# Weight additions, splits and first transposes on TensorE, and one planned schedule with two buffer sets

## The chip, the cores and the metric

The kernel runs on one core of one Trainium2 chip. The metric is the device time of one execution in microseconds; lower is better. Before the change three timed runs gave 585.99, 586.38 and 587.47 us, median 586.38. The engines are named as in the profile: PE is TensorE, DVE VectorE, ACT ScalarE, POOL GpSimd, SP the engine that issues the DMAs. PE, DVE, ACT, POOL and SP each work through their own list in order.

## The reference, cut to what matters

```python
# attention: q, k, v of (8, 8, 576, 64), f32; 4 heads local, 4 strided
scores = (1.0 / np.sqrt(D)) * np.matmul(q, k.transpose(0, 1, 3, 2))
mask_local = (rel >= 0) & (rel < 32)
mask_strided = (rel >= 0) & (pos[None, :] % 32 == pos[:, None] % 32)
scores = np.where(masks, scores, -1e9)
attn = softmax(scores)
x = np.matmul(attn, v)                  # then heads side by side: (8, 576, 512)
# gated MLP: w_in (512, 1024), conv_w (3, 1024), w_out (1024, 512)
h = np.maximum(x @ w_in, 0.0)
conv_out = sum(conv_w[k] * shifted(h, k - 1) for k in range(3))
gate = 1.0 / (1.0 + np.exp(-conv_out))
out = (h * gate) @ w_out
```

`w_in`, `conv_w` and `w_out` come as float64 and reach the chip as pairs of 32-bit words; the kernel makes f32 of them itself.

## The kernel before

The batches are computed one after another. Each batch has four attention pairs (two heads each), then `mm1` (x times `w_in`, eight blocks f of 128 columns, two halves of 288 tokens), the gating of each f, and `mm2` (times `w_out`, four blocks m of 128 columns). All big products are done in three terms of a high and a low part (`xh`/`xl`, `wih`/`wil`, `gh`/`gl`, `woh`/`wol`): 192 products in `mm1` and 192 in `mm2` of a batch, each 128 x 128 by 288 columns (L387, L426).

An attention pair: scores on PE (L307), maximum and subtraction on DVE (L319, L320), exp on ACT (L322), sum and reciprocal on DVE (L323, L325), the normalisation `pn` on POOL (L326), a transpose of 32 x 32 blocks, either by DVE into `tt` with ACT copies from there (L329, L341) or by DVE directly (L344), the values on PE (L350), and the split of the result into `xh` (ACT, L364) and `xl` (DVE, L365).

Sixteen weight blocks (eight of `w_in`, eight of `w_out`, 512 KB each) are converted from float64 by `convert` and `from_f64`: one ACT pass (L245), five DVE passes (L246 to L254), an addition of head and tail on POOL (L256), the high part on ACT (L277) and the low part as a subtraction (L280) on POOL or DVE, which `SPLIT_W` chooses for each block. Two buffers each hold the words, `wa` and `wt`. `gl` of each f is the same helper `split` (L280); `SPLIT_G` puts six of eight on POOL.

A planner sets the order. Each operation has an engine, a duration, a due time and the operations it depends on; `order` walks through time and takes, on each engine, the ready operation that is due first. It is called twice: first the four attentions of batch 0 with four buffer sets and PSUM regions of their own, with four `w_in` blocks; then the rest, with two buffer sets. The due times are the tables at the top (`FIRST_AT`, `W_IN_AT` and so on). The planner knows no sharing between engines and gives a transfer a fixed duration.

Of the kernel before, what the change touches and what calls it, by code (L numbers as in the profile page):

```python
# [19 lines left out]
P = 128  # L20
W = 32
# [3 lines left out]
WAIT = 0.1  # L25
ACT_PENALTY = 0
PE_PENALTY = 1

FIRST = "q0 q1 w0 q3 v1 w1 w2 q2 w3 v2 v3 c0 v0"
SETUP = ['vav', 'v', 'ava', 'v']  # L30
WARM = 4
WARM_SCORES = [2, 4, 2, 4]
WARM_VALUES = [0, 5, 0, 9]
FIRST_AT = [19.3, 22.4, 23.0, 26.9]
SECOND_AT = [11.6, 24.2, 37.3, 76.0]
LATER_AT = [31.8, 33.4, 39.2, 37.7]
START = 28.0
PERIOD = 70.0
MM1_STEP = 3.5
MM2_AT = 39.3  # L40
MM2_STEP = 22.4
LOAD_Q = 82.1
LOAD_V = 20.4
W_IN_AT = [-37.0, 3.8, 71.4, 61.1, 22.5, 42.2, 40.1, 48.5]
W_OUT_AT = [1.2, -51.9, 2.7, -37.4, 27.2, 25.2, 41.3, 30.0]
SPLIT_W = "pppppppvppvppvpv"
SPLIT_G = "vppvpppp"
FIRST_SCALE = "aavaaaav"
FIRST_GATE = "vppppvpp"


class Plan:
# [6 lines left out]
    def op(self, engine, dur, at, fn, reads=(), writes=(), chain=(), table=None):  # L59
        i = len(self.ops)  # L60
        deps = set(chain)
        for key in reads:
            if key in self.last_write:
                deps.add(self.last_write[key])
        for key in writes:
            deps.update(self.readers.get(key, ()))
            if key in self.last_write:
                deps.add(self.last_write[key])
        for key in reads:
            self.readers.setdefault(key, set()).add(i)  # L70
        for key in writes:
            self.last_write[key] = i
            self.readers[key] = set()
        deps.discard(i)
        self.ops.append((engine, dur, at, fn, deps, table))
        return i

    def order(self, free, done):
        ops = self.ops
        n = len(ops)  # L80
        left = [0] * n
        users = [[] for _ in range(n)]
        ready = [0.0] * n
        end = {}
        lo = len(done)
        for i in range(lo, n):
            for d in ops[i][4]:
                if d < lo:
                    ready[i] = max(ready[i], self.after(done[d], d, i))
                else:  # L90
                    left[i] += 1
                    users[d].append(i)
        pool = {}
        for i in range(lo, n):
            if not left[i]:
                pool.setdefault(ops[i][0], []).append(i)
        out = []
        while True:
            best = None
            for e, c in pool.items():  # L100
                if not c:
                    continue
                t = max(free.get(e, 0.0), min(ready[i] for i in c))
                def key(i):
                    sw = e == "act" and ops[i][5] not in (None, self.table) or e == "pe" and ops[i][5] != self.kind
                    return (ops[i][2] + (ACT_PENALTY if e == "act" else PE_PENALTY) * sw, i)
                cand = min((i for i in c if ready[i] <= t), key=key)
                for i in c:
                    if ready[i] > t and key(i) < key(cand) and ready[i] < t + min(WAIT, 0.9 * ops[cand][1]):
                        cand = i  # L110
                        t = ready[i]
                        break
                if best is None or t < best[0]:
                    best = (t, e, cand)
# [4 lines left out]
            if e == "act" and ops[i][5] not in (None, self.table):  # L119
                self.table = ops[i][5]  # L120
                t += 1.29
            if e == "pe" and ops[i][5] != self.kind:
                self.kind = ops[i][5]
                t += 0.087
            end[i] = t + ops[i][1]
            free[e] = end[i]
            out.append((t, i))
            for u in users[i]:
                ready[u] = max(ready[u], self.after(end[i], i, u))
                left[u] -= 1  # L130
                if not left[u]:
                    pool.setdefault(ops[u][0], []).append(u)
        out.sort()
        return [i for _, i in out], end

    def after(self, t, d, i):
        a, b = self.ops[d][0], self.ops[i][0]
        if a == "dma":
            return t + 0.92
        if b == "dma":  # L140
            return t + 1.25
        if a == b:
            return t if a == "pe" else t + 0.13
        if b == "pe":
            return t + 0.15
        return t + (0.2 if a == "pe" else 0.15 if a == "act" else 0.08 if a == "pool" else 0.2 if b == "pool" else 0.13)

    def emit(self, free, done):
        order, end = self.order(free, done)
        for i in order:  # L150
            self.ops[i][3]()
        done.extend(end[i] for i in range(len(done), len(self.ops)))
# [3 lines left out]
def tile_banded_attention_gated_mlp(ctx, tc, qT, kT, vw, w_in, conv, w_out, mask, ident, out):  # L156
    nc = tc.nc
    B, NHP, D, _, S = qT.shape
    DM, FF = w_in.shape
# [3 lines left out]
    NF = FF // P  # L163
    NM = DM // P
# [8 lines left out]
    def attention_buffers(pool, i):  # L173
        return (pool.tile([P, 2, S], F32, name=f"q{i}"), pool.tile([P, 2, SP], F32, name=f"k{i}"),
                pool.tile([96, 2, NU, D], F32, name=f"v{i}"), pool.tile([96, 2, NU, 64], F32, name=f"pt{i}"),
                pool.tile([P, NU, 65], F32, name=f"t{i}"), pool.tile([P, NU, 64], F32, name=f"pn{i}"),
# [4 lines left out]
    tt = const.tile([P, NU, 64], F32, name="tt")  # L181
# [6 lines left out]
    NW = 2  # L188
    words = [const.tile([P, 4, P, 2], I32, name=f"ws{i}") for i in range(NW)]
    wa = [const.tile([P, 4 * P], I32, name=f"wa{i}") for i in range(NW)]  # L190
    wt = [const.tile([P, 4 * P], I32, name=f"wt{i}") for i in range(NW)]
# [4 lines left out]
    def slot(n):  # L196
        return n if n < NHP else n % NB

    def load_q(n, at):
        i, b, hp = slot(n), n // NHP, HPS[n % NHP]  # L200
        q, k = buffers[i][:2]
        op(Q, 0.82, at, lambda: nc.sync.dma_start(out=q[0:D], in_=qT[b, hp]), (), [("q", i)])
        op(Q, 0.82, at, lambda: nc.sync.dma_start(out=k[0:D, :, W:], in_=kT[b, hp]), (), [("k", i)])

    def load_v(n, at):
        i, b, hp = slot(n), n // NHP, HPS[n % NHP]
        v = buffers[i][2]
        op(Q, 1.23, at, lambda: nc.sync.dma_start(out=v, in_=vw[b, hp]), (), [("v", i)])

    def set_up(i, at):  # L210
        q, k, v, pt, t = buffers[i][:5]
        es = SETUP[i]

        def copy(e, dst, src, key, dv, da):
            if e == "a":
                op(A, da, at, lambda: nc.scalar.copy(dst, src), ["small"], [key])
            else:
                op(V, dv, at, lambda: nc.vector.tensor_copy(out=dst, in_=src), ["small"], [key])

        op(G, 0.09, -1, lambda: nc.gpsimd.memset(k[0:D, :, :W], 0.0), (), [("kpad", i)])  # L220
        copy(es[0], q[D:].rearrange("p h (u c) -> p (h u) c", c=64),
             small[D:, 0].unsqueeze(1).to_broadcast([64, 2 * NU, 64]), ("qid", i), 0.67, 1.05)
        if i == 1:
            op(Q, 0.87, at, lambda: nc.sync.dma_start(out=k[D:], in_=mask), (), [("kmask", i, h) for h in range(2)])
        elif i == 3:
            op(A, 1.1, at, lambda: nc.scalar.copy(k[D:], buffers[1][1][D:]), [("kmask", 1, 0)], [("kmask", i, h) for h in range(2)])
        else:
            op(G, 0.34, at - 0.5, lambda: nc.gpsimd.tensor_copy(out=k[D:, :, S:], in_=small[D:, 1, :W].unsqueeze(1).to_broadcast([64, 2, W])),
# [330 lines left out]
```

## Time and profile before

| what | value |
|---|---|
| median of the timed runs | 586.38 us |
| profiled execution | 583.28 us, its span 581.5 us |
| PE busy | 523.2 us (90%) |
| DVE busy | 416.1 us (72%) |
| ACT busy | 348.6 us (60%) |
| POOL busy | 169.2 us (29%) |
| mean granted TensorE clock | 0.944 |
| moved by DMA | 52.19 MB, mean 90 GB/s |

The span runs from the first to the last instruction; some 1.8 us of the execution lie around it. A share over the span mixes stages: the slices of the page show a start of some 140 us with a TensorE clock of 0.5 to 0.9 in places, then a long stretch at full clock. A row of a group reads: line, engine, operation, out<-in, shape, count, busy us, mean ns, idle time before it and who ended that. A row of the waits reads: who waited, for whom, us in total, times, longest.

### The profile page before, as it was taken

How to read it: one execution, taken by the hardware profiler on the slowest of the kernel's cores; microseconds unless marked ns; L12 is line 12 of the kernel's file. 1: busy time of each engine (PE TensorE's matmuls, PEld its weight loads, DVE VectorE, ACT ScalarE, POOL GpSimd, SP SyncE). 2: the span in 40 equal slices, each digit the busy share in tenths (PEclk: the TensorE clock that was granted, in tenths of full speed). 3: DMA queues.
4: the chain of work that ended last, by engine and by line, in shares of the span. 5: the costliest groups of instructions: out<-in, count | busy, mean ns of one | idle time of the engine just before them, and what ended most of it. 6: DMA issues, size and time to landing. Idle time of an engine off the chain costs nothing.

```text
span 581.5 us, 15083 instructions
## 1 busy us (share of the span) xinstructions
PE 523.2 (90%) x6558; PEld 498.2 (86%) x6558; DVE 416.1 (72%) x587; ACT 348.6 (60%) x661; POOL 169.2 (29%) x148
## 2 busy tenths in 40 slices
PE   5468855798998999999999999999999999899997
PEld 2348854697997999999998999899999999799997
DVE  5596999998697666875787678767777668733830
ACT  4395685566676448663874477545765386535731
POOL 5434676674023111321033012311232103300220
PEclk9566967889999999999999999999999999999999
DMA  8994213445202460066006530355015600210001
GB/s 194 228 214 108 66 56 110 141 145 163 68 1 81 130 160 1 4 182 163 24 1 143 151 77 2 85 152 134 1 32 155 165 22 1 83 42 22 1 35 47
DMA packets 24178, 52.19 MB, mean 90 GB/s; under 512 B 2480, under 2 KB 10736, under 8 KB 24112
## 3 DMA queue, kind: packets, MB, share of 16 engines
q1 hardware_dynamic: 24112, 51.23, 33.0%
q8 instruction: 51, 0.84, 0.6%
q14 instruction: 15, 0.12, 0.1%
HBM read 41.79 MB, written 9.44 MB: 88 GB/s over the span
## 4 chain that ended last, share of the span: by engine, by line
PE 44%; DVE 22%; ACT 11%; issue 4%; POOL 0%; POOLq 0%; DVEq 0%; ACTq 0%
PE m L426 24%; PE m L387 13%; DVE c L404 8%; DVE c L409 6%; PE s L307 4%; ACT c L398 4%; ACT gh L277 2%; PE s L350 2%; ACT c L407 2%; DVE gl L280 1%; DVE wt L250 1%; DVE xl L365 1%; ACT pt L341 1%; ACT h L393 1%; ACT xh L364 1%
## 5 line engine op out<-in xcount | busy, mean ns | idle before, releaser
L387 PE MATMUL m<-xh,wil 128*128 128x288 f32 x512 | 153.1, 299 | 5.7 <-DVE wil L280 3.8
L426 PE MATMUL m<-gl,woh 128*128 128x288 f32 x512 | 153.7, 300 | 3.7 <-POOL gl L280 3.3
L426 PE MATMUL m<-gh,wol 128*128 128x288 f32 x512 | 152.6, 298 | 4.9 <-DVE wol L280 2.9
L426 PE MATMUL m<-gh,woh 128*128 128x288 f32 x512 | 155.5, 304 | 1.3 <-issue 1.3
L387 PE MATMUL m<-xh,wih 128*128 128x288 f32 x512 | 153.4, 300 | 2.0 <-DVE xl L365 1.5
L404 DVE SCALAR_TENSOR_TENSOR c<-h,cw,c 128x576 f32<-128x576 f32 x128 | 121.1, 952 | 44.7 <-ACT c L398 44.4
L387 PE MATMUL m<-xl,wih 128*128 128x288 f32 x512 | 153.1, 299 | 0.0
L280 POOL TENSOR_TENSOR gl<-c,gh 128x576 fp32r<-128x576 f32 x48 | 71.5, 1490 | 202.0 <-ACT gh L277 192.1
L426 PEld LDWEIGHTS m<-gl,woh 128*128 128x128 f32 x512 | 97.4, 190 | 9.1 <-POOL gl L280 7.5
L387 PEld LDWEIGHTS m<-xh,wil 128*128 128x128 f32 x512 | 98.2, 192 | 6.1 <-DVE wil L280 4.0
L426 PEld LDWEIGHTS m<-gh,wol 128*128 128x128 f32 x512 | 97.5, 190 | 4.0 <-DVE wol L280 3.4
L426 PEld LDWEIGHTS m<-gh,woh 128*128 128x128 f32 x512 | 97.3, 190 | 4.2 <-issue 1.5
L387 PEld LDWEIGHTS m<-xh,wih 128*128 128x128 f32 x512 | 98.2, 192 | 2.8 <-DVE xl L365 1.7
L387 PEld LDWEIGHTS m<-xl,wih 128*128 128x128 f32 x512 | 98.1, 192 | 0.0
L341 ACT COPY pt<-tt 32x288 f32<-32x288 f32 x160 | 68.8, 430 | 24.8 <-DVE tt L329 16.1
L326 POOL TENSOR_TENSOR pn<-t,sm 128x576 f32<-128x576 f32 x32 | 38.2, 1203 | 145.7 <-DVE sm L325 141.6
L277 ACT CAST gh<-c 128x576 fp32r<-128x576 f32 x64 | 43.0, 671 | 41.0 <-DVE c L409 39.3
L409 DVE TENSOR_TENSOR c<-h,c 128x576 f32<-128x576 f32 x58 | 54.7, 944 | 15.0 <-ACT c L407 14.1
L393 ACT ACTIVATE h<-m 128x288 f32<-128x288 f32 x128 | 50.5, 405 | 22.6 <-PE m L387 21.3
L432 ACT COPY o<-m 128x288 f32<-128x288 f32 x64 | 24.8, 398 | 58.5 <-PE m L426 54.2
L407 ACT ACTIVATE c<-c 128x576 f32<-128x576 f32 x64 | 43.4, 678 | 11.7 <-DVE c L404 11.0
L398 ACT ACTIVATE c<-h,cw 128x576 f32<-128x576 f32 x62 | 48.1, 775 | 1.5
(71 smaller groups left out, 590.2 us busy)
## 6 DMA issues: line engine op xcount, KB each, us to landing
v<-in_dram SPq DMA_DIRECT2D x32, 432.0 KB, 4.0
q<-in_dram SPq DMA_DIRECT2D x32, 288.0 KB, 5.0
k<-in_dram SPq DMA_DIRECT2D x32, 288.0 KB, 5.7
out_dram<-o SPq DMA_DIRECT2D x32, 288.0 KB, 2.2
ws<-in_dram SPq DMA_DIRECT2D x16, 512.0 KB, 3.7
k<-in_dram SPq DMA_DIRECT2D x1, 304.0 KB, 6.7
small<-in_dram SPq DMA_DIRECT2D x1, 32.0 KB, 2.1
cwords<-in_dram SPq DMA_DIRECT2D x1, 24.0 KB, 10.6
```

Source lines behind the costliest of these rows:

```text
L277: op(A, ta, at, lambda: nc.scalar.copy(hi(), src), [skey], [(key, "h")])
L280: lambda: eng.tensor_tensor(out=lo(), in0=src, in1=hi().bitcast(F32), op=ALU.subtract),
L326: op(G, 1.11, at + 5.5, lambda: nc.gpsimd.tensor_tensor(out=pn, in0=t, in1=sm.unsqueeze(2).to_broadcast([P, NU, 64]), op=ALU.mult), [("t", ...
L341: op(A, 0.333, at + 7.5, lambda dst=dst, j=j, p=p: nc.scalar.copy(dst, tt[j:j + 32, :, 32 * p:32 * p + 32]), ["tt"], [key])
L387: nc.tensor.matmul(ps, a[:, c, fs], x[:, c, tok], start=(n == 0 and m == 0), stop=(n == NC - 1 and m == 2))
L393: op(A, 0.291, at + 1.5 * t + 1.7, lambda ps=ps, t=t: nc.scalar.activation(out=h[:, 1 + t * H2:1 + t * H2 + H2], in_=ps, func=AF.Relu), [( ...
L398: op(A, 0.67, at + 3.6, lambda: nc.scalar.activation(out=c_, in_=h[:, 0:S], func=AF.Copy, scale=cw[:, f:f + 1]), kh + ["cw"], [kc])
L404: op(V, 0.73, at + 3.6 + 0.8 * kk, lambda kk=kk: nc.vector.scalar_tensor_tensor(out=c_, in0=h[:, kk:kk + S], scalar=cw[:, kk * NF + f:kk * ...
L407: op(A, 0.57, at + 6, lambda: nc.scalar.activation(out=c_, in_=c_, func=AF.Sigmoid), [kc], [kc], table=1)
L409: op(ge, 0.67 if ge == V else 1.36, at + 6.7, lambda: (nc.vector if ge == V else nc.gpsimd).tensor_tensor(out=c_, in0=h[:, 1:S + 1], in1=c ...
L426: nc.tensor.matmul(ps, a[:, f, ms], g[:, f, tok], start=(f == 0 and n == 0), stop=(f == NF - 1 and n == 2))
L432: op(A, 0.291, at + 3 * t + 3, lambda ps=ps, tok=tok: nc.scalar.copy(o[:, tok], ps), [("M", mi)], [("o", oi, t)])
```

## The change

Four things change together.

1. **Weights.** `_words` lays each weight block out in order, so that a row of a partition is 4 KB in one piece. There are three word buffers, two of `wa` and `wt`, one of the tail `wl`, and the first three `w_in` blocks land in `misc`, which later holds `h`, `c` and `o`. Head and tail are added by PE in PSUM: a product of the head with a unit matrix (f32), then one of the tail (f32r). For blocks marked "a" in `SPLIT_W` (10 of 16) PE also subtracts the high part, by four products with a negative unit matrix, and ACT copies the low part out; for the others DVE subtracts.
2. **First transposes.** For the four pairs of batch 0 and the first two of batch 1 the normalised probabilities go into `pad`, 18 products with a unit matrix transpose them into PSUM (`turn`), and three ACT copies bring them to `pt`, zeros with them.
3. **GpSimd** keeps the normalisation, in place, and `gl` of two in eight f (one in batch 0).
4. **One plan.** Everything is planned at once, with two buffer sets throughout, PSUM regions `psR` for attention and `mm`, a lock between DVE and POOL, a TensorE that is slow after a pause, transfers by their bytes, new durations and new due times.

```diff
+PASSES = 0
+AHEAD = 4.0
+RATE = 205.0
-SPLIT_W = "pppppppvppvppvpv"
-SPLIT_G = "vppvpppp"
+SPLIT_W = "aavvvaaaaaaaavvv"
+SPLIT_G = "vvvpvpvv"
+FIRST_SPLIT_G = "vvvvvpvv"
+TURNED = 2
+FIRST_GATE = "vvvvvvvv"
...
+                if ops[i][6]:
+                    lock["dve"] = end[i] + 0.03
+                    lock["pool"] = end[i]
...
+    NWS, NWA, NWT, NWL = 3, 2, 2, 1
...
     def slot(n):
-        return n if n < NHP else n % NB
+        return n % NB
...
-        op(G, 0.2 if short else 1.23, at, lambda: nc.gpsimd.tensor_tensor(out=w, in0=w, in1=af, op=ALU.add), [ka], [kt])
...
+        def whole():
+            nc.tensor.matmul(ps, eye, t, start=True, stop=False)
+            nc.tensor.matmul(ps, eyer, tail, start=False, stop=not last)
+        op(A, 0.615, at, lambda: nc.scalar.copy(hi(), parts(t)), [kt], [(key, "h")])
+        op(T, 1.1, at, whole, [kt, kl, "unit", "eyer"], [("M", mi)], table=4)
+        if last:
+            def rest():
+                for x in range(4):
+                    nc.tensor.matmul(ps[:, P * x:P * x + P], negr, hi()[:, x, :], start=False, stop=x == 3)
+            op(T, 0.3, at, rest, [(key, "h"), "negr"], [("M", mi)])
+            op(A, 0.59, at, lambda: nc.scalar.copy(lo(), parts(ps)), [("M", mi)], [(key, "l")])
+        else:
+            op(V, 0.69, at, lambda: nc.vector.tensor_tensor(out=lo(), in0=parts(ps), in1=hi().bitcast(F32), op=ALU.subtract),
+               [("M", mi), (key, "h")], [(key, "l")])
...
+        def turns():
+            for u in range(n_u):
+                for e in range(2):
+                    o = ps[0:96, 128 * u:128 * u + 128].rearrange("p (h x) -> p h x", h=2)[:, :, 32 * e:32 * e + 32]
+                    nc.tensor.matmul(o, pad[:, u0 + u, 32 - 32 * e:128 - 32 * e], unit[:, e, :], start=True, stop=True)
...
+        turned = spread is None
+        pn = pad[:, :, 32:96] if turned else t
...
+def _words(w, n):
+    y = np.ascontiguousarray(w).view(np.int64).reshape(n, 4, P, -1, P)
+    return np.ascontiguousarray(y.transpose(3, 0, 2, 1, 4).reshape(-1, P, 4 * P))
```

**SP, the loads of batch 0 from the third pair on.** Before, every pair has its own set (58, 66, 98 and 106 are q of the four sets):

```order
L202 DMA q_98<-in_dram 64x1152
L203 DMA k_99<-in_dram 64x2x576
L208 DMA v_100<-in_dram 96x1152
L272 DMA ws_81<-in_dram 128x4x256
L208 DMA v_108<-in_dram 96x1152
L260 DMA cwords<-in_dram 128x48
L208 DMA v_60<-in_dram 96x1152
```

After it the same queue, from the load of `q` of pair 3 into set 1 (65 to 67) to the last `v` of batch 0:

```order
L312 DMA q_65<-in_dram 64x1152
L317 DMA k_66<-in_dram 64x2x576
L312 DMA q_58<-in_dram 64x1152
L317 DMA k_59<-in_dram 64x2x576
L322 DMA v_60<-in_dram 96x1152
L377 DMA ws_98<-in_dram 128x1024
L377 DMA ws_99<-in_dram 128x1024
L312 DMA q_65<-in_dram 64x1152
L322 DMA v_67<-in_dram 96x1152
```

The last `v` of batch 0 now stands behind q and k of batch 1's first pair, the next weight blocks and q of its second pair; 24 other loads (8024 KB) are ahead of it.

**PE, around the first product of `mm1`.** Before, the values of the last two pairs, then `mm1` (m_550 is its first PSUM buffer):

```order
L350 MATMUL sF_116<-pt_101,v_100 64x64 x18
L350 MATMUL sF_117<-pt_109,v_108 64x64 x18
L387 MATMUL m_550<-xh,wih 128x288
L387 MATMUL m_550<-xh,wil 128x288
L387 MATMUL m_550<-xl,wih 128x288
```

After the change the same place, with additions (L393, L394; r_95 and r_96 hold the buffers of `mm`), transposes (L439) and values (L508) between:

```order
L393 MATMUL r_96<-wt_103,eyes 128x512
L394 MATMUL r_96<-wl_104,eyer 128x512
L508 MATMUL r_95<-pt_61,v_60 64x64 x18
L439 MATMUL r_93<-eyes,pad 96x2x32 x16
L545 MATMUL r_95<-xh,wih 128x288
L545 MATMUL r_95<-xh,wil 128x288
L545 MATMUL r_95<-xl,wih 128x288
L439 MATMUL r_93<-eyes,pad 96x2x32 x2
L393 MATMUL r_96<-wt_102,eyes 128x512
L394 MATMUL r_96<-wl_104,eyer 128x512
L508 MATMUL r_93<-pt_68,v_67 64x64 x18
```

The first products of `mm1` moved ahead of the last pair's values, and each weight block puts two products into PE's list, each of which waits for a DVE result; all blocks use the one tail buffer wl_104.

**POOL, from the gating of batch 0 on.** Before (49 onwards of its list; wt are the converted words, wil and wol low parts):

```order
L409 TENSOR_TENSOR c_541<-h_538,c_541 128x576
L326 TENSOR_TENSOR pn_63<-t_62,sm_65 128x576
L280 TENSOR_TENSOR gl<-c_541,gh 128x576
L280 TENSOR_TENSOR wil<-wt_86,wih 128x4x128
L409 TENSOR_TENSOR c_542<-h_539,c_542 128x576
L256 TENSOR_TENSOR wt_85<-wt_85,wa_83 128x512
L280 TENSOR_TENSOR gl<-c_542,gh 128x576
L280 TENSOR_TENSOR wil<-wt_85,wih 128x4x128
```

After the change POOL's list for the whole of that stage (the fifth and sixth pairs into `pad`, one `gl`, the last two pairs in place; the last row's second is the first pair of batch 2):

```order
L479 TENSOR_TENSOR pad<-t_62,sm_64 128x9x64
L479 TENSOR_TENSOR pad<-t_69,sm_71 128x9x64
L417 TENSOR_TENSOR gl<-misc,gh 128x576
L479 TENSOR_TENSOR t_69<-t_69,sm_71 128x9x64
L479 TENSOR_TENSOR t_62<-t_62,sm_64 128x9x64 x2
```

Additions, low parts and gates left POOL's list; the additions went to PE, the gates and most `gl` to DVE.

More of the change, by code (lines that the diff above doesn't have):

```diff
@@ new lines, in attention @@
+        if not turned and sum(spread):
+            op(V, 0.777, at + 6.8, lambda: nc.vector.transpose(out=tt, in_=pn), [("t", i)], ["tt"])
+        keys = []
+        if turned:
+            keys = [("pt", i, 0, 0, 0), ("pt", i, 0, 0, 1), ("pt", i, 0, 1, 0)]
+            turn(n, full, ks[0], 0, 4, keys[0], at + 7)
+            turn(n, full[:, 512:], ks[1], 4, 4, keys[1], at + 7.6)
+            turn(n, full, ks[0], 8, 1, keys[2], at + 8.2)
+            keys += [("pt", i, h, e, p) for h in range(2) for e in range(2) for p in range(2) if ("pt", i, h, e, p) not in keys]
@@ L333, in attention @@
+        for h in range(0 if turned else 2):
             for e in range(2):
@@ L377, in mm1 @@
         h, c_ = hs[hi], cs[hi]
+        sg = FIRST_SPLIT_G[f] if early else SPLIT_G[f]
         for t in range(2):
```

559 lines of the change are left out of this document (326 added, 233 removed).

## The prediction, as put on record before the run

> **What bounds the kernel now.** I read the windows first, cut at the first `mm1` product (48.04 us) and at the first `mm1` product of batch 1 (149.11 us). Columns: busy time of each engine with its instructions, granted clock, DMA share, GB/s.
>
> ```profile
> core 0: us, PE busy (x) PEld busy (x) DVE busy (x) ACT busy (x) POOL busy (x), PEclk, DMA share, GB/s
> 0.00:48.04 48.04, 26.28 (x462) 17.72 (x463) 31.13 (x55) 28.54 (x55) 22.72 (x40) 0.66 0.86 203
> 48.04:149.12 101.08, 78.80 (x961) 73.60 (x962) 95.11 (x120) 62.40 (x118) 59.42 (x44) 0.84 0.38 111
> 149.12:581.50 432.38, 418.11 (x5138) 406.92 (x5136) 289.84 (x413) 257.67 (x489) 87.03 (x65) 1.00 0.27 72
> 10.00:40.00 30.00, 16.21 (x312) 11.51 (x314) 20.72 (x39) 18.05 (x37) 11.81 (x11) 0.54 0.99 230
> ```
>
> There are three stages with three limits. From 10 to 40 us the DMA engines are full (share 0.99, 230 GB/s). From 48 to 149 VectorE is busy 95.1 of 101.1 us. After 149 TensorE is busy 418 of 432 us. The waits of TensorE say what is left there, in the third stage and then in the second:
>
> ```profile
> PE s L307 <- DVE xl L365: 3.9, 6, 0.7
> PE m L426 <- issue: 2.8, 2, 1.5
> PE m L426 <- POOL gl L280: 2.8, 9, 1.0
> ...
> PE s L350 <- ACT pt L341: 8.8, 4, 5.0
> PE m L387 <- DVE wil L280: 3.8, 1, 3.8
> PE s L307 <- DVE xl L365: 3.3, 2, 2.4
> PE m L426 <- DVE wol L280: 2.9, 2, 2.6
> PE m L387 <- POOL wil L280: 1.8, 1, 1.8
> ```
>
> The third stage has some 10 us of waits in 432. The second has 23.6 (the rows shown and four small ones), and more is lost to half clock and to a VectorE that GpSimd holds up. The timeline shows the holding:
>
> ```profile
> 67.67 1.92 POOL L280 TENSOR_TENSOR gl<-c,gh 128x576 fp32r<-128x576 f32 x1
> ...
> 68.25 1.63 DVE L246 TENSOR_SCALAR wa<-wa 128x512 f32<-128x512 f32 x1
> ...
> L246 DVE TENSOR_SCALAR wa<-wa x16: 407/424/1630, 13.0 to 133.9; 128x512 f32<-128x512 f32 x16
> L248 DVE TENSOR_SCALAR wa<-wa x16: 385/427/1628, 14.0 to 134.8; 128x512 int32<-128x512 int32 x16
> L250 DVE SCALAR_TENSOR_TENSOR wt<-ws,wa x16: 677/834/1901, 14.5 to 136.7; 128x512 int32<-128x512 int32 x16
> L252 DVE TENSOR_SCALAR wa<-wt x16: 368/416/1530, 15.8 to 138.4; 128x512 int32<-128x512 int32 x16
> L254 DVE SCALAR_TENSOR_TENSOR wa<-ws,wa x16: 675/683/1755, 16.2 to 138.8; 128x512 f32<-128x512 uint32 x16
> L404 DVE SCALAR_TENSOR_TENSOR c<-h,cw,c x16: 800/806/1856, 56.4 to 113.5; 128x576 f32<-128x576 f32 x16
> L409 DVE TENSOR_TENSOR c<-h,c x2: 742/1223/1704, 62.6 to 96.7; 128x576 f32<-128x576 f32 x2
> ```
>
> A clamp that takes 407 ns alone took 1630 ns when it began during a GpSimd pass; the last rows give shortest/median/longest in ns. GpSimd is busy 59 us of that stage.
>
> **Part 1, the first 48 us.** The loads are the limit. Counted from SP's order, the last `v` of batch 0 stands behind 8456 KB (8.66 MB) in the new kernel: the same q, k and v, six weight blocks, and q and k of batch 1's first pairs. The stream reaches that amount when 10 to 40 us have gone by at 230 GB/s and the first 10 us at the row below:
>
> ```profile
> 0.00:10.00 10.00, 6.59 (x88) 3.19 (x88) 5.31 (x8) 3.58 (x4) 7.57 (x26) 1.00 0.75 166
> ...
> L341 ACT COPY pt<-tt 32x288 f32<-32x288 f32 x68 | 29.2, 429 | 7.6 <-DVE tt L329 6.7
> ...
> 48.04 0.61 PE L387 MATMUL m<-xh,wih 128*128 128x288 f32 x1 [1.52 <-DVE xl L365]
> ```
>
> 1.66 + 6.9 = 8.56 MB by 40 us, so 8.66 MB at about 40.4. Behind it come the values (1.1 to 2.2 us), the xh copy and the xl subtraction: full `mm1` from about **44** instead of 48.04. The weights now come in rows of 4 KB, which no row prices; between no gain and the same bytes 20% faster lie 0 to 3 us, and I take none. The two buffer sets instead of four make q, k and v wait for earlier pairs; the tightest is `v` of pair 3, which SP issues after the values of pair 1; by the chain of that pair (q and k landed, softmax, transposes: about 32 us) 1.5 MB of earlier issues, some 7 us, are then still under way, so these waits are hidden under the transfers. Without that cover each would cost its own length. Eight ScalarE copies of 0.43 us a pair become three from PSUM, which no row shows; priced between none and the eight they replace they save at most 3.4 us a pair, hidden under the same loads.
>
> **Part 2, from 44 us to `mm1` of batch 1.** With the additions and splits on TensorE, GpSimd keeps in this stage only four normalisations and one `gl`. VectorE's list there (102 rows) at the shortest durations above: ten conversions of 0.407 + 0.385 + 0.677 + 0.368 + 0.675 = 2.51 us are 25.1; 16 convolution passes of 0.80 are 12.8; 36 other full passes (gates, `gl`, `lo`, softmax, xl, transposes) at 0.742 are 26.7; small ones 1.2; together 66 us, plus about 7 us held by the five GpSimd passes (1.2 to 1.9 each): 73 us, where 95 were. So VectorE stops being the bound, and TensorE becomes it. Its list goes by these rows (chain and timeline):
>
> ```profile
> 525.59 12.74 PE m L387 x96
> 499.31 2.22 PE s L307 x144
> 513.60 2.25 PE s L350 x72
> ...
> 146.62 0.40 PE L426 MATMUL m<-gh,woh 128*128 128x288 f32 x1
> 146.85 0.30 PE L426 MATMUL m<-gh,wol 128*128 128x288 f32 x1
> 146.99 0.29 PE L426 MATMUL m<-gl,woh 128*128 128x288 f32 x1
> ```
>
> A product is 12.74/96 = 0.1327 us; two scores take 2.22, two values 2.25; a change of type costs about 0.1 (0.23 to the next start instead of 0.13). No row shows the new matmuls. Values write 64 partitions and cost 2.25/36 = 0.0625 us for 64 f32 columns, scores write 32 and cost half of it, so I take a full-width one at 0.125 per 64 columns; below stands 0.0625. The addition is then 8 x 0.125 + 512/288 x 0.1327 = 1.24 us (low end 0.74), a split 0.24, a transpose 0.125. From 44 us: 375 products 49.8, six scores 6.7, four values 4.5, 36 transposes 4.5, 11 additions 13.6, eight splits 1.9, some 50 changes of type 5.0: **86 us** (78 at the low end). Three us of waits, the choice between none and the 23.6 of before, nearer to none because the conversions run well ahead, give 44 + 86 + 3 = **133** in place of 149.1: 16 us gained. What hides the new 25 us on TensorE is that it stood still or at half clock for them; without that cover they would be paid in full.
>
> The Trainium skill ("FP8 and Floating Point Precision", TensorE Precision Notes) says that true FP32 takes four passes through the array; four times 0.236 us would make an addition's f32 half an estimated 0.94 us, which speaks for the upper end and would take 0.7 us off the sum; no run shows it yet.
>
> **Part 3, the other seven batches.** The products are the same, and scores now stand further behind the values whose xl they wait for, and six of eight `gl` are on VectorE. Of 3.9 + 2.8 of such waits I take 4 us; the bounds are 0 and 8.
>
> **Sum.** 583.3 (the profiled execution: 581.5 and 1.8 around it) - 16 - 4 = 563.3. The three timed runs have their median 3.1 above the profiled one, so the forecast is **566**.
>
> **Rivals.** *VectorE stays the bound.* If its list is stretched as before (L404 took 1126 ns on average there, 1.4 times the shortest), 66 becomes 92 us; then 44 + 92 and some 6 us for the last values and products give 142, and 583.3 - 7 - 4 + 3 = 575. For it: GpSimd still has work; against: 5 passes instead of 44 instructions.
>
> ```profile
> L404 DVE SCALAR_TENSOR_TENSOR c<-h,cw,c 128x576 f32<-128x576 f32 x16 | 17.9, 1126 | 0.7 <-ACT c L398 0.7
> ```
>
> *Half clock stays.* After waits TensorE ran at half clock:
>
> ```profile
> 115.54 0.61 PE L426 MATMUL m<-gh,wol 128*128 128x288 f32 x1 [2.63 <-DVE wol L280]
> 115.95 0.44 PE L426 MATMUL m<-gl,woh 128*128 128x288 f32 x1
> 116.19 0.44 PE L426 MATMUL m<-gh,woh 128*128 128x288 f32 x1
> ...
> 117.00:121.00 4.00, 4.00 (x19) 4.00 (x18) 3.96 (x5) 3.02 (x5) 4.00 (x3) 0.50 0.18 63
> ```
>
> Products 0.24 apart until 121 us: a wait of 2.6 us cost some 2.7 more. At the old mean clock of 0.84, 86 us become 102, the end 149, and the time 582. Against: the conversions fill TensorE's pauses. The Trainium skill ("TensorE: Matmul & The Clock Gate", What's actually happening) lets the clock fall only after an idle window of about 3.4 us; by it this wait would have been free, but the trace shows that it was not, and the trace decides.
>
> *More than forecast.* Transposes and additions at the low end (-8), loads 3 us sooner, no waits (-3), 8 us later on: 583.3 - 30 - 8 + 3 = 548. For it: all engines have room once GpSimd is out of the way.
>
> *Slower.* TensorE works in order, and there is one buffer `wl` for the tail of a weight block: an addition that waits for VectorE holds every product behind it, and VectorE's next tail waits for that addition. At 2.9 us (the wait on `wol` above) for each of 11 conversions it would be 32 us, and 598; it decides from (20 + 0.3% of 586)/11 = 2.0 us each. Against: before, TensorE's waits on weights shown above are four, in 16 conversions.
>
> **How the numbers follow.** Forecast 0.56 (558 to 573), VectorE 0.13 and half clock 0.09 (573 to 583), more 0.15, slower 0.05, nothing 0.02. The range 552 to 580 leaves out half of "more", the slower end and a little of the second. A measurement of this kernel tells about 0.3% from no change; faster 0.92, same 0.03 (the last and a sliver of the half-clock case), slower 0.05.
>
> **What would show it.** Part 1: the first full `mm1` at 41 to 46 us with the loads at 0.9 and more before it. Part 2: VectorE below 85% and TensorE above 90% busy from there to `mm1` of batch 1, which begins between 128 and 138; L351 (L250 before) with its median near 0.69 us instead of 0.83; additions of 0.7 to 1.3 us. Part 3: 424 to 432 us from there to the end. Wrong would be: loads that stand still in the first 40 us, long waits of TensorE for `wl`, or a clock below 0.9 in the second stage.

## The result, and the profile after

| | before | changed |
|---|---|---|
| time, median | 586.18 us (584.05 to 587.47, 4 runs) | 623.15 us (620.79 to 624.90, 4 runs) |
| ratio to before | | 1.063 (95%: 1.058 to 1.068) |
| profiled execution, its span | 583.28, 581.5 us | 622.13, 620.2 us |
| first full `mm1` | 48.04 | 54.35 |
| from there to `mm1` of batch 1 | 101.1 | 95.1 |
| from there to the end | 432.4 | 470.8 |

The forecast was 566 us; the kernel became 6.3% slower. The windows of the changed kernel, cut at the same places (the first `mm1` product after the last values of batch 0, and the first of batch 1), and two cuts in the start; columns as before:

```profile
0.00:54.35 54.35, 37.62 (x616) 29.86 (x616) 31.03 (x63) 20.63 (x37) 7.61 (x23) 0.94 0.78 194
54.35:149.44 95.09, 88.37 (x1098) 78.02 (x1095) 69.42 (x116) 59.85 (x110) 6.33 (x6) 1.00 0.41 110
149.44:620.20 470.76, 432.31 (x5138) 408.82 (x5136) 291.22 (x444) 261.80 (x493) 45.05 (x38) 1.00 0.25 67
10.00:40.00 30.00, 23.69 (x433) 18.56 (x430) 16.38 (x37) 9.74 (x19) 3.87 (x9) 0.89 0.86 212
25.00:30.00 5.00, 3.75 (x48) 2.46 (x49) 2.78 (x9) 0.88 (x2) 1.15 (x1) 0.50 0.68 142
```

The second stage is as forecast in kind: VectorE 69.4 of 95.1 us, TensorE 88.4. The loss is in the third, where TensorE has the same 5138 instructions and 38 us more. Its waits there, in the changed kernel:

```profile
PE r L545 <- ACT misc L551: 25.6, 51, 0.5
PE r L585 <- ACT misc L591: 7.7, 15, 0.5
PE r L459 <- issue: 1.2, 1, 1.2
```

66 waits of 0.5 us for ScalarE's copy out of PSUM, of a kind that the waits of before do not have. One of them in the timeline (start, duration, engine, line; in brackets the idle time and what ended it):

```profile
218.43 0.30 PE L545 MATMUL r<-xl,wih 128*128 128x288 f32 x1
218.56 0.29 PE L545 MATMUL r<-xh,wih 128*128 128x288 f32 x1
218.69 0.29 PE L545 MATMUL r<-xh,wil 128*128 128x288 f32 x1
218.82 0.29 PE L545 MATMUL r<-xl,wih 128*128 128x288 f32 x1
219.15 0.41 ACT L551 ACTIVATE misc<-r 128x288 f32<-128x288 f32 x1 [0.73 <-PE r L545]
219.62 0.40 PE L545 MATMUL r<-xh,wih 128*128 128x288 f32 x1 [0.50 <-ACT misc L551]
219.85 0.29 PE L545 MATMUL r<-xh,wil 128*128 128x288 f32 x1
```

The group for t = 0 ends with the product at 218.43. ScalarE's ReLU of that group could start at about 218.75, but starts at 219.15, right after the third product of the *next* group (218.82 + 0.29); and the fourth product of that group waits until the ReLU has ended. Two groups that share no element of PSUM wait for each other, both ways. From 218.82 to 219.85 pass 1.03 us for two steps that otherwise take 0.13 each: 0.77 us lost.

What the two groups share is a tile. The kernel before had four `mm` buffers that were PSUM tiles of their own; in the changed one they are halves of two tiles of 1024 columns (`psM` from `psR[2]` and `psR[3]`). The waits written into the program show the same. In the pair of groups below, which fills the two halves of `r_96`, the wait for ScalarE (Activation_49) stands at the fourth product of the second group:

```
962 L545 MATMUL r_96<-xh,wih 128x288
963 L545 MATMUL r_96<-xh,wil 128x288
964 L545 MATMUL r_96<-xl,wih 128x288
965 L545 MATMUL r_96<-xh,wih 128x288 [waits Activation_49]
```

The other direction stands there too. TensorE counts up a semaphore (a counter on which other engines wait), and in this pair it does so only at the third product of the second group, by 15: for the twelve products of the first group and these three. The ReLU of the first group waits for that count, so it cannot start when its own group ends. In the program with tiles of their own (below) `mm1` counts up at the twelfth product of a group.

### The profile page after: what moved, and what is told of

It reads as the page before. It is cut to its first block, busy times and chain, and to the rows that moved or that the text cites. A ratio compares the mean times of both kernels' runs of the same rounds, so it can differ in the third digit from the quotient of the medians.

```text
span 620.2 us, 15601 instructions
## 1 busy us (share of the span) xinstructions
PE 558.3 (90%) x6846; PEld 516.7 (83%) x6846; DVE 391.7 (63%) x622; ACT 342.3 (55%) x639; POOL 59.0 (10%) x66
## 4 chain that ended last, share of the span: by engine, by line
PE 86%; ACT 8%; DMA 3%; issue 2%; DVE 0%; POOL 0%; SPq 0%; ACTq 0%; POOLq 0%
PE r L545 34%; PE r L585 33%; PE r L508 6%; PE r L459 5%; ACT misc L551 4%; PE r L439 3%; PE r L393 2%; DMA q<-in_dram 2%; ACT misc L591 1%; DMA misc<-in_dram 1%; PE r L400 1%; PE r L394 1%; ACT t L473 1%; ACT pt L441 0%; ACT misc L557 0%
## 5 line engine op out<-in xcount | busy, mean ns | idle before, releaser
L545 PE MATMUL r<-xh,wih 128*128 128x288 f32 x512 | 157.2, 307 | 28.9 <-ACT misc L551 27.6
L585 PE MATMUL r<-gh,woh 128*128 128x288 f32 x512 | 156.3, 305 | 9.1 <-ACT misc L591 8.2
L585 PE MATMUL r<-gh,wol 128*128 128x288 f32 x512 | 150.9, 295 | 0.2 <-issue 0.2
L545 PE MATMUL r<-xl,wih 128*128 128x288 f32 x512 | 150.8, 294 | 0.0
L545 PE MATMUL r<-xh,wil 128*128 128x288 f32 x512 | 150.7, 294 | 0.0
L585 PE MATMUL r<-gl,woh 128*128 128x288 f32 x512 | 150.7, 294 | 0.0
L563 DVE SCALAR_TENSOR_TENSOR misc<-misc,cw 128x576 f32<-128x576 f32 x128 | 104.5, 821 | 52.1 <-ACT misc L557 51.0
L585 PEld LDWEIGHTS r<-gh,wol 128*128 128x128 f32 x512 | 96.1, 188 | 0.4 <-issue 0.4
L545 PEld LDWEIGHTS r<-xh,wil 128*128 128x128 f32 x512 | 96.1, 188 | 0.1
L545 PEld LDWEIGHTS r<-xl,wih 128*128 128x128 f32 x512 | 96.1, 188 | 0.0
L459 PE MATMUL r<-k,q 128*32 128x64 f32 x2304 | 39.1, 225 | 11.6 <-DMA q<-in_dram 8.2
L479 POOL TENSOR_TENSOR t<-t,sm 128x576 f32<-128x576 f32 x26 | 29.8, 1155 | 192.4 <-DVE sm L476 182.9
```

The lines of the kernel that those rows point to most:

```text
L459: nc.tensor.matmul(ps[j:j + 32, 64 * u:64 * u + 64], q[:, h, W * s:W * s + W], k[:, h, W * s:W * s + 64], start=True, stop=True, tile_posi ...
L479: op(G, 1.152, at + 5.5, lambda: nc.gpsimd.tensor_tensor(out=pn, in0=t, in1=sm.unsqueeze(2).to_broadcast([P, NU, 64]), op=ALU.mult), [("t" ...
L545: nc.tensor.matmul(ps, a[:, c, fs], x[:, c, tok], start=(n == 0 and m == 0), stop=(n == NC - 1 and m == 2))
L563: op(V, 0.811, at + 3.6 + 0.8 * kk, lambda kk=kk: nc.vector.scalar_tensor_tensor(out=c_, in0=h[:, kk:kk + S], scalar=cw[:, kk * NF + f:kk ...
L585: nc.tensor.matmul(ps, a[:, f, ms], g[:, f, tok], start=(f == 0 and n == 0), stop=(f == NF - 1 and n == 2))
```

## Experiments on the third stage

Theory A: the layout in halves makes these waits, and they are the loss. Rivals: B, ScalarE empties the buffers too late whatever their layout; C, products get slower while ScalarE reads.

**Halves apart.** The order on every engine stays; from batch 1 on neighbouring groups get halves of different tiles.

```diff
-    NWS, NWA, NWT, NWL = 3, 2, 2, 1
+    NWS, NWA, NWT, NWL, MI = 3, 2, 2, 1, [0, 2, 1, 3]
... (in `mm1` and in `mm2`)
-            ps = psM[mi][:, :H2]
+            ps = psM[MI[mi] if b else mi][:, :H2]
```

> Edit: from batch 1 on, the second and third of the four mm buffers change places, so that two neighbouring groups of products never write halves of one PSUM tile; the order on every engine stays as in the changed kernel. Theory A (false waits between the halves of one PSUM tile): after the changed kernel's first mm1 product of batch 1, TensorE waits 66 times for ScalarE's copy out of the other half (51 by L551, 15 by L585), and each costs 0.77 us (1.03 us between three starts that are else 0.26 apart). Without them the stretch from there to the end falls from 470.6 to about 420 us (415 to 432), the time to about 571 (565 to 585), and those rows vanish from TensorE's waits. Rival B (the plan itself is the loss: ScalarE frees the mm buffers too late whatever tile they lie in): the waits stay, under another buffer, and the time stays at 612 to 623. Rival C (ScalarE reading while TensorE writes costs the product itself): the waits go but products take longer than 0.133 us from start to start, and the stretch ends near 445. All three: mm1 of batch 1 begins at 149 to 150 us as before, since batch 0 is untouched.

Measured: 579.88 us (578.35 to 580.78, 4 runs), ratio to before 0.991 (95%: 0.988 to 0.994). The last stage, its waits:

```profile
144.76:576.40 431.64, 420.01 (x5138) 407.75 (x5136) 290.80 (x444) 258.91 (x493) 47.35 (x38) 1.00 0.27 73
```

```profile
PE r L545 <- ACT misc L551: 3.1, 7, 0.5
PE r L545 <- ACT misc L591: 1.5, 3, 0.5
PE r L459 <- issue: 1.3, 1, 1.3
PE r L585 <- issue: 0.8, 1, 0.8
PE r L585 <- ACT misc L591: 0.6, 1, 0.6
```

55 of the 66 waits are gone and the stage is 39.1 us shorter, 0.71 us for each. 11 remain; with tiles of their own, below, they go as well. The stage ended at the upper end expected, since I had counted on all 66. B falls, as the waits went with the layout. C falls too, as a product takes what it took (median 0.295 us in both kernels). That mm1 of batch 1 began at 144.76 and not at 149 is in none of the theories; the repeated runs below take it up.

**The kernel before, with halves.** The same layout put into the kernel before the change, and nothing else:

```diff
-        psM = [psum.tile([P, 512], F32, name=f"m{i}") for i in range(NPM)]
+        psP = [psum.tile([P, 1024], F32, name=f"m{i}") for i in range(NPM // 2)]
+        psM = [psP[i // 2][:, i % 2 * 512:i % 2 * 512 + 512] for i in range(NPM)]
```

> Edit: the kernel before the change, with its four mm buffers laid out as halves of two PSUM tiles, nothing else. Theory A: TensorE gets waits for ScalarE's ReLU once per f and once per pair of mm2 groups, 66 to 70 after mm1 of batch 1 at 0.5 us of idle each, and the stretch from there to the end rises from 432.4 by 40 to 51 us; the time rises to 622 to 640. Rivals B and C (not the layout): the time stays at 583 to 590.

Measured: 628.01 us (one run). Its last stage and waits:

```profile
150.49:626.20 475.71, 430.82 (x5138) 408.38 (x5136) 289.56 (x413) 260.53 (x489) 86.69 (x65) 1.00 0.24 66
```

```profile
PE m L387 <- ACT h L393: 24.9, 49, 0.8
PE m L426 <- ACT o L432: 7.7, 15, 0.5
```

64 waits and 475.7 us in place of 432.4, that is 43.3 us or 0.68 for each. The layout alone does to the old kernel what the change did to it.

**Tiles of their own.** All four buffers as separate tiles, in every batch. They take the place of two of the four tiles of 1024 columns, which leaves two attention regions instead of three.

```diff
-    psR = [psum.tile([P, 1024], F32, name=f"r{i}") for i in range(4)]
-    psM = [psR[2 + i // 2][:, i % 2 * 512:i % 2 * 512 + 512] for i in range(NPM)]
+    psR = [psum.tile([P, 1024], F32, name=f"r{i}") for i in range(2)]
+    psM = [psum.tile([P, 512], F32, name=f"m{i}") for i in range(NPM)]
...
-        return (0, 1, 2, 0)[n] if n < NHP else n % 2
+        return n % 2
```

> Edit: as the changed kernel, but each of the four mm buffers is a PSUM tile of its own, in all batches; the eight banks then leave two regions for attention instead of three, so the scores of pair 2 of batch 0 wait for the values of pair 0. Theory A: the 11 waits of TensorE that e1_halves_apart still has after mm1 of batch 1, and the 5 before it, go too; each was worth 0.71 us (39.0 us for the 55 that went), so the stretch from mm1 of batch 1 to the end falls from 431.6 to about 424 us (420 to 428). The start is paid by the shared region: scores of pair 2 some 3 to 6 us later, mm1 of batch 1 at 144 to 150. Time 568 to 578. Rival B (ScalarE is late by itself): the waits appear again under other buffers and the stretch stays at 429 to 434.

Measured: 572.18 us (572.06 to 576.34, 4 runs), ratio to before 0.978 (95%: 0.972 to 0.984): faster than both kernels, though the interval leaves open whether by 2%. The second and third stage, a stretch of the second, and the last stage's waits:

```profile
42.12:146.84 104.72, 99.29 (x1176) 87.59 (x1173) 77.09 (x133) 68.50 (x123) 8.58 (x7) 0.95 0.44 120
146.84:569.90 423.06, 416.08 (x5138) 407.49 (x5136) 287.37 (x438) 256.68 (x488) 46.10 (x37) 1.00 0.27 73
50.00:62.00 12.00, 10.86 (x86) 10.61 (x87) 3.28 (x7) 4.55 (x10) 1.15 (x1) 0.57 0.40 105
```

```profile
PE r L459 <- issue: 1.3, 1, 1.3
PE m L585 <- issue: 1.1, 1, 1.1
PE r L508 <- DVE pt L502: 0.9, 3, 0.3
```

No wait for a copy is left; 423.1 us where 424 was expected and 432.4 stood before the change. (470.76 - 423.06)/66 = 0.72 us for each wait. The three edits give one price, 0.68 to 0.72.

The cut at 42.12 us is not the point that the other tables call the first full `mm1`. With two regions the values of the last pair of batch 0 come only at 51.69, and `mm1` has some products ahead of them; the first product behind them is at 58.95. The runs below that build on this one are cut in the same way, ahead of the last pair. In the stretch from 50 to 62 us the granted clock was 0.57.

The Trainium skill ("Perfetto Trace Analysis", Matmuls) asks that independent groups of products rotate through different PSUM banks, so that a copy out of one lies beside the products of the next. No run here shows how the buffers lie in the banks. In both kernels the four buffers are 512 columns each and are used in turn, and with halves of one tile TensorE still waited; what these runs show is that the buffers must also be different tiles.

**GpSimd's part in the last stage.** Before the change six of eight `gl` were GpSimd's; now two are.

```diff
-SPLIT_G = "vvvpvpvv"
+SPLIT_G = "vppvpppp"
```

> Edit: as e5_tiles_apart, but after batch 0 the low parts of g are split by GpSimd for six of the eight f as before the change, instead of two. Theory J (the 9 us by which the stretch from mm1 of batch 1 to the end is shorter than before the change, 423.1 against 432.4, come from GpSimd's late gl and the late xl): the stretch grows to 427 to 433, and TensorE's waits for POOL gl are back with some 3 us. Rival L (they come from elsewhere, the order of scores and products or the copies): 421 to 425, no such waits. Start unchanged within 1 us in both, if the clock is granted alike.

Measured: 577.49 us (one run); the last stage and all its waits:

```profile
151.25:575.70 424.45, 417.64 (x5138) 409.47 (x5136) 277.72 (x410) 257.79 (x488) 79.76 (x65) 0.99 0.27 73
```

```profile
PE r L459 <- issue: 3.0, 1, 3.0
```

Rival L: the stage is 1.4 us longer, and no wait for GpSimd's `gl` returns. The 9 us that this stage gains over the kernel before are thus not won by moving `gl`: the waits for xl (3.9 us) and for `gl` (2.8) of before went with other parts of the change, which no run here tells apart. The later start (151.25) is another matter: the first products in a row came at 46.40 in that execution, 4.3 us later than the 42.12, after transposes at half speed (5.27 us instead of 2.85).

## Experiments on the start

Theory D: in the start TensorE's own list is the bound. Rival E: the loads are, with the two buffer sets.

**No transposes on TensorE**, on top of the halves apart (pairs go through VectorE and ScalarE as before the change, the zeros of `pt` written once):

```diff
...
-            attention(j, FIRST_AT[j], None)
+            attention(j, FIRST_AT[j], [1, 1, 1, 1])
...
-                    attention(n, at, (None if j < TURNED else [1, 1, 1, 1]) if early else [1, 0, 0, 1])
+                    attention(n, at, [1, 1, 1, 1] if early else [1, 0, 0, 1])
```

> Edit: as e1_halves_apart, and no pair is transposed on TensorE; VectorE and ScalarE transpose as before the change, with zeros written once. Theory D (the start is bound by TensorE's list, in which a pair's 18 transposes take 3.3 us and one wait of 0.7 for ScalarE's copy, not the 2.25 us I took): the first mm1 product of three blocks in a row comes well ahead of the 54.4 us of the changed kernel, at 44 to 49, and mm1 of batch 1 at 135 to 144 instead of 149.6. Rival E (the loads are the bound: with two buffer sets q waits for the scores, and v for the values, of the pair two before): first mm1 stays at 52 to 55, mm1 of batch 1 at 146 to 152. Rival F (VectorE becomes the bound again with eight pairs of transposes): mm1 of batch 1 later than 152.

Measured: 584.93 us (one run). Three blocks of products in a row stand at 43.20 already, but they belong to the earlier pairs; the values of the last pair come at 48.71 and the full `mm1` at 51.98, later than the 49.67 with the transposes on TensorE. Batch 1 begins at 148.85, with one pair's attention still to come (180 TensorE instructions more behind it). TensorE had 29.8 us of work in those 52, with the DMA engines at 0.87:

```profile
0.00:51.98 51.98, 29.82 (x551) 21.76 (x551) 36.59 (x72) 30.34 (x59) 10.31 (x27) 0.90 0.87 214
```

Taking this work away from TensorE gains nothing, and `mm1` of batch 1 lies where E has it. That does not make the loads the bound: the transposes went to VectorE and ScalarE, and from 35 to 40 us these two are full and the DMA engines are not:

```profile
35.00:40.00 5.00, 4.41 (x118) 4.06 (x119) 4.86 (x12) 4.80 (x11) 0.00 (x0) 0.66 0.39 125
```

Of TensorE's waits between 18 and 52 us one of 2.5 us ends on a load, and 7.3 us end on VectorE or ScalarE.

**Every transpose of batch 0 twice**, on top of the halves apart:

```diff
-                    nc.tensor.matmul(o, pad[:, u0 + u, 32 - 32 * e:128 - 32 * e], unit[:, e, :], start=True, stop=True)
+                    for _ in range(2 if n < NHP else 1): nc.tensor.matmul(o, pad[:, u0 + u, 32 - 32 * e:128 - 32 * e], unit[:, e, :], start=True, stop=True)
```

> Edit: as e1_halves_apart, and every transposing product of batch 0's four pairs is done twice (same result, same order). One pair's turns take 3.6 us, so TensorE's list in the start grows by about 13 us. Theory D (TensorE's list, in order, is the bound from the first turn on): the first full mm1 (49.67 us in e1_halves_apart) moves by 10 to 14 us, to 60 to 64, and mm1 of batch 1 (144.76) by 8 to 14. Rival E (loads and the two buffer sets are the bound, TensorE has room): both move by less than 4 us.

Measured: 593.07 us (one run), first full `mm1` at 61.34, batch 1 at 156.47.

```profile
0.00:61.34 61.34, 47.24 (x760) 40.44 (x761) 31.09 (x63) 20.39 (x37) 7.56 (x23) 1.00 0.68 172
```

TensorE has 11.4 us more to do (47.24 for 35.82) and both points move by 11.7, or by 10.0 against the second execution of the halves apart (below). Added work counts nearly in full, as D has it. With the run above: TensorE's list is in front, and VectorE and ScalarE would take its place if they got the transposes.

**Addition without the tail**, on top of the halves apart.

```diff
             nc.tensor.matmul(ps, eye, t, start=True, stop=not last)
-            nc.tensor.matmul(ps, eyer, tail, start=False, stop=not last)
```

> Edit: as e1_halves_apart, with the product of the tail left out of each addition, so that the low bits of the weights are missing; 16 products less at 0.6 to 0.7 us (1.2 at half clock), 5 of them before the first full mm1. Theory D: the first full mm1 comes 3 to 5 us before 49.67, mm1 of batch 1 8 to 11 us before 144.76, at 134 to 137. Rival E: first full mm1 within 1.5 us of 49.67. Rival G (from the first mm1 on something other than TensorE's list binds, the conversions on VectorE or the loads): mm1 of batch 1 within 5 us of 144.76 whatever the start does.

Measured: 578.62 us (one run), first full `mm1` at 52.62, batch 1 at 145.44. The step between came out at 92.82 us in place of 95.09, 2.3 us less, where TensorE's work fell by 2.5 (85.93 for 88.38). By the numbers expected this speaks for G, but the edit took away less than I had thought. The timeline around one addition, with the tail (halves apart) and without:

```profile
33.51 1.12 PE L393 MATMUL r<-wt,eyes 128*128 128x512 f32 x2
34.08 0.80 PE L394 MATMUL r<-wl,eyer 128*128 128x512 f32 x1
34.72 0.37 PE L514 MATMUL r<-warm 128*128 128x224 bf16 x2
```

```profile
37.13 1.12 PE L393 MATMUL r<-wt,eyes 128*128 128x512 f32 x2
38.09 0.36 PE L514 MATMUL r<-warm 128*128 128x224 bf16 x2
```

An addition takes 1.21 us with its tail and 0.96 without: 0.25 for the tail, not 0.6 to 0.7, and 11 of them are 2.8. Stage and list moved alike, which agrees with D; the start itself ran at half speed between two points (a turn took 5.38 us there, not 2.93), so it says nothing.

**Order of the first loads**, on top of the halves apart:

```diff
-FIRST = "w0 k0 q0 v0 k1 w1 q2 q1 v1 k2 c0 w2 w3 q3 k3 v3 v2 w4"
+FIRST = "k0 q0 v0 k1 q1 w0 v1 w1 q2 k2 c0 w2 w3 q3 k3 v2 v3 w4"
```

> Edit: as e1_halves_apart, and the order of the first loads changes: q, k, v of pair 0 and q, k of pair 1 ahead of the first two weight blocks (in the changed kernel a weight block is first, and q of pair 1 lands at 18.0 us). Rival E (loads are the bound of the start): the first scores come about 2 us and those of pair 1 about 5 us earlier, and the first mm1 product of three blocks in a row 3 to 6 us before 54.4; mm1 of batch 1 at 144 to 147. Theory D (TensorE's list is the bound): what TensorE has to do is the same, and little changes, 52 to 55 and 147 to 151.

Measured: 591.77 us (one run). The scores began at 7.18 and 12.95 us, 1.3 and 3.3 earlier; the first full `mm1` came at 52.71, as D has it, and batch 1 at 154.40, later than either theory allows and with one pair's attention still to come. The first transposes then waited 3.1 us for GpSimd's normalised probabilities and ran at half speed, and the additions moved behind them. The due times belong to one order of loads; this run separates nothing.

**Additions and splits by GpSimd**, on top of the separate tiles:

```diff
...
-        op(A, 0.615, at, lambda: nc.scalar.copy(hi(), parts(t)), [kt], [(key, "h")])
-        op(T, 1.1, at, whole, [kt, kl, "unit", "eyer"], [("M", mi)], table=4)
+        op(G, 1.23, at, lambda: nc.gpsimd.tensor_tensor(out=t, in0=t, in1=tail.bitcast(F32), op=ALU.add), [kl], [kt], lock=True)
+        split(hi, lo, parts(t), at, kt, key, OLD_SPLIT_W[c], 0.615, 0.69, 1.23, True)
+        return
...
```

`OLD_SPLIT_W` gives GpSimd 12 of the 16 low parts and VectorE four, not 11 and five, so 28 passes.

> Edit: as e5_tiles_apart, but head and tail of the 16 weight blocks are added by GpSimd as before the change, ScalarE takes the high part from that sum, and 11 of the 16 low parts are subtracted by GpSimd, five by VectorE. TensorE loses about 23 us of work ahead of mm1 of batch 1 (16 additions at some 1.15 us, 10 splits at 0.45), GpSimd gains 27 passes of 1.2 to 1.9 us. Theory H (the additions were worth moving: what GpSimd does holds VectorE up): mm1 of batch 1 comes later than the 146.84 us of e5_tiles_apart, at 150 to 165, VectorE's clamps and shifts show longest durations above 1.5 us again. Rival I (TensorE's list is the bound, so its 23 us count): mm1 of batch 1 at 130 to 140. Rival K (the two balance): within 3 us of 146.84.

Measured: 593.93 us (one run), batch 1 at 170.65.

```profile
47.60:170.65 123.05, 95.50 (x1178) 90.95 (x1175) 89.81 (x137) 68.72 (x123) 39.53 (x29) 0.79 0.42 114
```

Theory H, beyond its range: 24 us later, and VectorE's shifts take up to 1.4 to 1.6 us again. GpSimd is busy 39.5 us instead of 8.6, VectorE 89.8 instead of 77.1, and TensorE, with less to do, runs at a mean clock of 0.79. The due times were set for TensorE's additions, so part of the 24 us may be theirs; no run tells how much.

**Later pairs through VectorE**, on top of the separate tiles: `TURNED = 0` in place of 2.

> Edit: as e5_tiles_apart, but only batch 0's pairs are transposed on TensorE; the first two pairs of batch 1 go through VectorE and ScalarE as before the change. TensorE loses two pairs' turns, 36 transposes or 6.8 us, between the first full mm1 (42.12 us) and mm1 of batch 1 (146.84). Theory D (TensorE's list is the bound there: 99.3 of 104.7 us busy): mm1 of batch 1 some 4 to 8 us earlier, 139 to 143, and the time 564 to 568. Rival M (VectorE and ScalarE, which get the transposes and eight more copies, become late, and TensorE waits or loses its clock): mm1 of batch 1 at 145 to 152, time 570 to 578.

Measured: 570.19 us (one run; 572.06 in the profile of the separate tiles). Batch 1 begins at 143.20, but one pair's scores and values now stand behind that point and the last stage takes 425.0. TensorE's work fell by 5.3 us in all and the time by 1.9; waits for ScalarE's `wol` grew from 0.7 to 5.7 us. The four runs of the separate tiles lie 4.3 us apart, so the 1.9 decide nothing between D and M; the longer waits are M's.

**The changed kernel and the halves apart, once more**, on one chip:

> The changed kernel itself, profiled a second time on another chip, to see whether the 4.7 us by which its first full mm1 (54.35 us) came later than that of e1_halves_apart (49.67, same program up to there) belong to the one profiled execution (a wait of 2.19 us for nothing that the profile shows, and half clock behind it). Chance: the first full mm1 at 49 to 52 this time, and the stretch from mm1 of batch 1 to the end at 470 to 475. Not chance: first full mm1 again at 53.5 to 55.

> e1_halves_apart once more, beside the run above on the same chip. Chance: its first full mm1 lies anywhere from 49 to 55 us, as the waits and the clock of the start fall; the stretch from mm1 of batch 1 to the end is 431 to 433 as in the first run, 39 us less than in the changed kernel.

Measured: 622.58 and 580.04 us (one run each). First full `mm1` at 53.03, between the two ranges, and 51.38; the last stage 472.6 and 431.5 us. So the same program up to there reached its first full `mm1` at 54.35, 53.03, 51.38 and 49.67 us in four executions. Two things make the difference. The scores of the second pair (pair 1, counted from 0) stand behind TensorE's first waits for loads, and began at 18.00, 16.61, 17.52 and 16.20 us. From there to the first full `mm1` it took 36.4 us in both executions of the changed kernel and 33.9 and 33.5 in those of the halves apart: in the first two, half clock followed a wait that the profile puts down to nothing (the last section). The 39 to 41 us of the last stage are steady.

## Why the prediction was wrong, step by step

By its own sum the profiled execution should have taken 563.3 us; it took 622.13, 59 more. They are 10.4 in the first step, 6.1 in the second and 42.4 in the third.

- **Part 3 failed, and with it the forecast.** "The products are the same": they are, but the buffers that they write are not. The sum took 4 us of old waits off this stage and put new ones at nothing. I went through the waits that would go (xl, `gl`) and did not ask of the new `psM` line which copies it would tie to which products. 66 waits at 0.72 us are 47.5 us; with tiles of their own the stage takes 423.1, below the 424 to 432 of the forecast.
- **Part 1: the load limit was not in front any more.** "First full mm1 from about 44": 49.7 to 54.4. I put everything that TensorE does before that point under the loads. In the changed kernel TensorE waits for a load for the last time just before 18.00 us (`q` of pair 1). Of the 10.4 us, 2.5 are half clock after a wait (36.4 us against 33.9 with an equal wait, above). From 18.00 us on TensorE's own list sets the pace: it is busy 31.3 of the 36.45 us up to the first full `mm1`, and these are all its waits:

```profile
17.90:54.35 36.45, 31.32 (x533) 25.55 (x533) 22.79 (x47) 15.86 (x31) 3.73 (x6) 0.91 0.72 192
```

```profile
PE r L439 <- ACT pt L441: 2.8, 4, 0.8
PE r L459 <- issue: 2.2, 1, 2.2
PE r L459 <- DMA q<-in_dram: 0.3, 1, 0.3
```

- **The waits for buffers were not hidden under the transfers either.** SP, which issues the loads, waited in the first 54.35 us for TensorE's scores and values, seven times:

```profile
SPq L312 <- PE r L459: 15.1, 4, 7.3
SPq L322 <- PE r L508: 10.7, 3, 4.8
```

  `v` of pair 3, the tightest case by the prediction, was issued at 41.01 us, behind the values of pair 1, and not at about 32. The DMA engines fell to a share of 0.68 between 25 and 30 us. No product of TensorE waited for one of these loads, so this cost nothing here; after 18 us the loads followed TensorE, and not TensorE the loads.
- **Mis-sized in both: the transposes.** Taken at 0.125 us; these rows of the changed kernel say 2.93/16 = 0.18 (x32 counts each of the 16 products twice), and each pair stops for ScalarE's copy before its last two:

```profile
40.90 2.93 PE L439 MATMUL r<-eyes,pad 128*96 128x64 f32 x32
44.56 0.55 PE L439 MATMUL r<-eyes,pad 128*96 128x64 f32 x4 [0.73 <-ACT pt L441]
```

  From 40.90 to 44.95, where the next work starts, a pair costs 4.05 us in place of 2.25: 7.2 us for the four pairs of the start, 3.6 for the two after it.
- **Part 2 was right in kind.** VectorE 73% busy, TensorE 93%, `L351` at a median of 0.69 us, additions at 1.1 to 1.2 (taken: 1.24), clock 1.00, TensorE's list 88.4 us (taken: 86). That the list is so near is partly luck: the transposes were taken 3.6 us too small, and other terms too large. The waits were 6.7 instead of 3, of them four for ScalarE's ReLU by the same layout (2.0 us idle).
- **The addition was right.** Taken at 1.24 us with 0.74 as the low end, it measured 1.21, and 0.96 without the tail. The 0.96 stand by the estimate of 0.94 from the four passes of the Trainium skill ("FP8 and Floating Point Precision", TensorE Precision Notes).
- **The rivals.** VectorE as the bound and a lasting half clock did not come. "Slower" came, by another mechanism than the one tail buffer: in the second stage of the changed kernel no product of TensorE waited for `wl`, and the weight loads of the tail's products (L394) waited 2.4 us in all, never over 0.2. What it had right is that TensorE works in order and a short wait in its stream is paid each time: 66 times.

That the tile decides is shown three times, and the program says how: its waits are set for the tile as a whole, so two halves that share no element are ordered against each other.

## What to carry to other kernels

When a change lays buffers out anew, list for each wait in the new program which tile it guards: two buffers that are filled and emptied in turn belong in separate PSUM tiles, not in halves of one. A gap that repeats once per group on the bound engine, with an end that falls on another engine's copy, is the sign of it. And the list of the engine that gets the work has to be added up for the start as well: work that fills pauses is free only until the pauses are full.

## What was unexpected of the hardware

The clock of TensorE does not follow from the length of one wait. In the changed kernel a wait of 2.19 us amid the scores of pair 2 was followed by half clock, and in its second run one of 1.86; in the second run of the halves apart a wait of 2.15 us at the same place was not:

```profile
26.25 1.49 PE L459 MATMUL r<-k,q 128*32 128x64 f32 x44 [2.19 <-issue]
27.67 2.08 PE L393 MATMUL r<-wt,eyes 128*128 128x512 f32 x2
```

```profile
25.73 0.86 PE L459 MATMUL r<-k,q 128*32 128x64 f32 x44 [2.15 <-issue]
26.52 1.12 PE L393 MATMUL r<-wt,eyes 128*128 128x512 f32 x2
```

The same 44 instructions take 1.49 or 0.86 us. The Trainium skill ("TensorE: Matmul & The Clock Gate", What's actually happening) says that the clock is set by a window that runs freely, and does not start with the kernel. Then pauses of one length could end differently, but no run here shows where the windows lie. By its idle window of about 3.4 us none of these waits would have been long enough for half clock, but after 1.86 us half clock was there.
